# A gated feed-forward stage in token blocks of 384 instead of 256, with its inner features in pieces of 128

## The chip, the cores and the metric

The kernel runs on one core of a Trainium2 chip. The metric is the device time of one execution in microseconds (us). The core has TensorE (matmul; PE in the profile, its weight load PEld), VectorE (DVE), ScalarE (ACT), GpSimd (POOL) and SyncE (SP), whose queue issues every DMA of this kernel. Each engine works its own instructions in the order in which they stand in the program, and waits for others by semaphores.

## The reference

Three layers follow one another on 4 x 576 = 2304 tokens of width 512.

```
out_d     = softmax attention over q, k, v averaged over 4 neighbours   (144 x 144 per head)
out_local = softmax attention of each token on its 7 nearest tokens
x   = out_local + out_d repeated 4 times          -> 2304 x 512
xn  = x / sqrt(mean(x*x) + 1e-6) * rms_g
h   = silu(xn @ w_gate) * (xn @ w_val)            w: 512 x 1536
y   = h @ w_out                                   1536 x 512
r   = relu(y @ w_in)                              512 x 2048
out = (r * r) @ w_out2                            2048 x 512
```

## The kernel before

Every large product is made of three matmuls: an operand is split into a high part rounded to fp32r (names ending in h or hi) and the rest (l or lo), and high x high, high x low and low x high are summed in PSUM. The weights come as 64-bit words and are decoded in halves of 512 columns (`decode`): about four instructions on VectorE, two on ScalarE, two on GpSimd for each half.

The program has three overlapping parts.

Attention. `down` (16 pairs of heads, letters d in PLAN) is the averaged attention. `wide` and `wide_post` (a and b) do the local attention of batch 0 in 6 pieces of 96 tokens on TensorE. The other three batches' local attention is done by GpSimd and VectorE in 14 units of up to 128 tokens (`attend`, letter u): products `pr<-k,q` and `pr<-v,es`, of 128x896, one for each of 4 token rows, sums `sc` and `xa` on VectorE, the softmax `es` between them. `post` (letter p) adds the averaged part, takes the norm (squares on ScalarE, a small matmul `t<-ss,on`, a power `ms<-ms,half` on GpSimd), turns the unit (`t<-id,xa`) and splits it into the tiles xh and xl that the next stage reads.

First stage (w_gate, w_val, w_out). The tokens come in 9 blocks of 256, the inner features in 6 parts of 256. A step x (`hidden`, then `outp` of the step before) is one block and one part: 24 matmuls of 256 columns into bank g (two halves of 128 features side by side), `th` = tanh on ScalarE and one VectorE instruction on it; 24 matmuls into bank v, then `v<-v,th` on VectorE, `hh` on ScalarE, `hl<-v,hh` on VectorE; 24 matmuls from hh and hl into the block's two output banks, which are the pair a or the pair b in turn. There are 54 steps, 3888 matmuls. The first twelve steps take blocks 0 and 1 by turns (SEQ). After a block `y_out` copies its banks to SBUF and sends them to DRAM.

Second stage (w_in, w_out2): four blocks of 512 tokens and one of 256, each in 16 pieces of 128 features. Its matmuls have 512 columns.

Order. The functions only record instructions. `Plan.trace` then sets the order on each engine: it simulates the recorded instructions forth and back for ROUNDS rounds with fixed costs (`cost`, `lag`), seeds the priorities with SEED, and keeps the best round; PLAN is the order in which things are recorded, TAGS names the PSUM banks, SLOT the weight buffers. Where several engines may do an instruction (the engine names VP, AV, VPA) the same simulation picks one. Until the first matmul of the first stage it also fills TensorE's planned pauses with idle matmuls (`v<-id`, line 466 before). All instructions are issued from one line, 473 before (472 after), so tiles name them.

Of the kernel before, what the change touches and what calls it, by code (L numbers as in the profile page):

```python
# [29 lines left out]
RUNS = 32  # L30
# [11 lines left out]
BN = 256  # L42
# [21 lines left out]
SEED = 1  # L64
# [412 lines left out]
def attn_moe_kernel(ctx: ExitStack, tc, qs, kw, vw, qt, kt, vt, v4, wg, wv, wo, w2i, w2o, gw, gb,  # L477
# [7 lines left out]
    seq1 += [(j, fp) for j in range(len(set(SEQ)), len(BLK)) for fp in range(NP1)]  # L485
# [13 lines left out]
    def bank(tag, dtype=F32):  # L499
        return tile("ps", tag, [128, 512], dtype, 2 if tag in "ab" else 1)  # L500
# [42 lines left out]
    def decode(src, n, hi, lo, st, how="--"):  # L543
# [20 lines left out]
        if how[1] == "3":  # L564
            hf = low.bitcast(F32)
# [613 lines left out]
```

## Time and profile before

| what | value |
|---|---|
| median of 3 runs | 1001.02 us (1000.61 to 1002.26) |
| the profiled execution | 1000.25 us, span 998.0 us, mean granted clock 0.998 |
| TensorE busy | 980.2 us (98%), 6866 matmul records |
| VectorE busy | 587.6 us (59%) |
| ScalarE busy | 417.0 us (42%) |
| GpSimd busy | 442.3 us (44%) |

2.25 us of the execution lie outside the span of the trace. A matmul's own duration in the profile (307 ns for one of 256 columns) holds its way through the array; the next one starts earlier, so the cost of a matmul is read from how long a row of them takes. An fp32 matmul (attention) stands in the trace as two records, one of the first and second stage as one.

### The profile page before, as it was taken

What the parts mean: (1) busy time and instruction counts of PE and PEld (TensorE: products, weight loads), DVE (VectorE), ACT (ScalarE), POOL (GpSimd) and SP (SyncE); (2) the same over time, 40 slices, a digit from 0 to 9 for tenths busy, and PEclk for the clock granted to TensorE, in tenths of its full rate; (3) what the DMA queues carried; (4) which work ended last, traced back from release to release, by engine and by line L of the source; (5) the groups of instructions that cost most, each with busy time, mean ns of one, the idle gap of its engine ahead of it and who ended that gap; (6) DMA issues with size and microseconds to landing.
All of it is one profiled execution on the core that took longest, in us unless ns stands there. A gap on an engine that the chain in (4) does not pass through costs nothing.

```text
span 998.0 us, 17246 instructions
## 1 busy us (share of the span) xinstructions
PE 980.2 (98%) x6866; PEld 906.4 (91%) x6866; DVE 587.6 (59%) x985; ACT 417.0 (42%) x984; POOL 442.3 (44%) x298
## 2 busy tenths in 40 slices
PE   7998999999999999999999999999999999999998
PEld 7888999999999999999999998888888888888897
DVE  6999899786687857575634568963222322322232
ACT  5787665532435342323244557663222212322232
POOL 2566688867656676676733465863001000100000
PEclk9999999999999999999999999999999999999999
DMA  9954553253262523222011446334000100100010
GB/s 282 262 160 157 175 179 103 73 151 113 85 182 80 171 78 115 93 65 96 28 33 60 132 128 209 104 109 137 1 1 1 54 0 1 43 1 1 1 43 22
DMA packets 38465, 92.93 MB, mean 93 GB/s; under 512 B 4218, under 2 KB 14498, under 8 KB 38386
## 3 DMA queue, kind: packets, MB, share of 16 engines
q1 hardware_dynamic: 38386, 91.84, 29.6%
q8 instruction: 54, 0.88, 0.4%
q14 instruction: 25, 0.20, 0.1%
HBM read 80.62 MB, written 11.21 MB: 92 GB/s over the span
## 4 chain that ended last, share of the span: by engine, by line
PE 89%; DVE 5%; POOL 2%; DMA 2%; issue 1%; ACT 1%; SPq 0%; DVEq 0%; POOLq 0%; ACTq 0%
PE v L473 25%; PE g L473 24%; PE a L473 20%; PE b L473 15%; DVE b L473 2%; PE d L473 2%; DVE st L473 2%; PE t L473 2%; PE v L466 1%; DMA b<-in_qt 1%; DMA st<-in_wg 1%; POOL w L473 0%; POOL st L473 0%; POOL pr L473 0%; POOL b L473 0%
## 5 line engine op out<-in xcount | busy, mean ns | idle before, releaser
L473 PE MATMUL g<-xh,w 128*128 128x256 f32 (+1 forms) x776 | 176.8, 307 | 0.4 <-DVE th L473 0.4
L473 PE MATMUL v<-xh,w 128*128 128x256 f32 (+1 forms) x632 | 147.6, 311 | 0.5 <-DVE hl L473 0.5
L473 DVE SCALAR_TENSOR_TENSOR v<-v,th 128x512 f32<-128x512 f32 (+1 forms) x94 | 63.3, 674 | 128.6 <-ACT th L473 101.3
L473 PEld LDWEIGHTS g<-xh,w 128*128 128x128 f32 x776 | 131.1, 191 | 7.0 <-ACT xh L473 0.6
L473 ACT ACTIVATE th<-g 128x512 f32<-128x512 f32 (+1 forms) x94 | 54.5, 580 | 198.1 <-PE g L473 194.8
L473 POOL TENSOR_TENSOR pr<-v,es 128x896 f32<-128x896 f32 x54 | 99.4, 1939 | 65.7 <-DVE es L473 28.2
L473 PE MATMUL v<-xh,b 128*128 128x256 f32 (+1 forms) x552 | 123.9, 303 | 0.1
L473 POOL TENSOR_TENSOR pr<-k,q 128x896 f32<-128x896 f32 x54 | 115.4, 2158 | 9.6 <-DVE sc L473 7.2
L473 PE MATMUL g<-xl,w 128*128 128x256 f32 (+1 forms) x388 | 118.3, 305 | 0.1
L473 PEld LDWEIGHTS v<-xh,w 128*128 128x128 f32 x632 | 107.7, 191 | 7.1 <-PE g L473 0.7
L473 POOL TENSOR_TENSOR xl<-st,xh 128x1024 fp32r<-128x1024 f32 (+1 forms) x10 | 21.6, 2179 | 184.7 <-ACT xh L473 184.7
L473 PE MATMUL v<-xl,w 128*128 128x256 f32 (+1 forms) x316 | 97.9, 310 | 0.0
L473 PEld LDWEIGHTS v<-xh,b 128*128 128x128 f32 x552 | 93.0, 191 | 4.4 <-PE g L473 0.3
L473 PE MATMUL g<-xh,b 128*128 128x256 f32 (+1 forms) x408 | 94.4, 310 | 0.2 <-DVE th L473 0.2
L473 ACT CAST hh<-v 128x512 fp32r<-128x512 f32 (+1 forms) x94 | 53.5, 569 | 81.6 <-DVE v L473 71.3
L473 PE MATMUL v<-xl,b 128*128 128x256 f32 (+1 forms) x276 | 83.1, 301 | 0.0
L473 DVE SCALAR_TENSOR_TENSOR g<-g,th 128x512 f32<-128x512 f32 (+1 forms) x40 | 25.8, 645 | 95.5 <-ACT th L473 95.4
L473 DVE TENSOR_TENSOR hl<-v,hh 128x512 fp32r<-128x512 f32 (+1 forms) x94 | 62.4, 664 | 26.3 <-ACT hh L473 24.6
L473 PEld LDWEIGHTS g<-xl,w 128*128 128x128 f32 x388 | 74.1, 191 | 3.6 <-DVE xl L473 0.3
L473 POOL TENSOR_TENSOR st<-st 128x512 int32<-128x512 int32 x48 | 55.9, 1166 | 41.5 <-DVE st L473 39.4
L473 PEld LDWEIGHTS g<-xh,b 128*128 128x128 f32 x408 | 69.1, 190 | 4.2 <-issue 0.3
L473 ACT ACTIVATE st<-st 128x512 int32<-128x512 uint32 (+1 forms) x96 | 64.7, 684 | 18.7 <-DVE st L473 11.2
(207 smaller groups left out, 2336.8 us busy)
## 6 DMA issues: line engine op xcount, KB each, us to landing
k<-in_kw SPq DMA_DIRECT2D x12, 640.0 KB
v<-in_vw SPq DMA_DIRECT2D x12, 640.0 KB
st<-in_w2i SPq DMA_DIRECT2D x14, 512.0 KB
st<-in_w2o SPq DMA_DIRECT2D x14, 512.0 KB
y<-vv SPq DMA_DIRECT2D x18, 256.0 KB
out<-xh SPq DMA_DIRECT2D x18, 256.0 KB
st<-y SPq DMA_DIRECT2D x8, 512.0 KB
st<-in_wg SPq DMA_DIRECT2D x7, 512.0 KB
```

The source lines that it names most:

```text
L466: self.nc.tensor.matmul(out=out, lhsT=one, rhs=one, start=True, stop=True)
L473: getattr(self.hw[on[op]], method)(*args, **kw)
```

## The change

The first three blocks keep 256 tokens, the other 1536 tokens come in four blocks of 384 (BLK, UNITS). For a block of 384 a step is cut in two pieces of 128 features: 12 matmuls of 384 columns into bank g, 12 into v, 12 into the output, with tanh, hh, hl and the VectorE instructions of 128x384. A block's output takes four banks, both a and both b, and is copied one bank at a time into the staging ring "st", or for the last block into one tile; a block that crosses a multiple of 512 tokens is sent in two DMAs. `post` now handles one unit: 14 norms of up to 4 columns where there were 7 of up to 8. `th` has one buffer instead of two. The special forms of `decode` (low word in a PSUM bank) are gone. PLAN, TAGS, SLOT, ROUNDS and SEED have new values, so the order on every engine differs; one pair of heads in `down` (tag dtdp) now sums k by four matmul groups instead of a VectorE sum.

```diff
--- before.py
+++ after.py
-UNITS = {2: [[(1, 0, 4)], [(1, 16, 2)]], 3: [[(1, 4, 4)], [(1, 8, 4)]], 4: [[(1, 12, 4)], [(2, 0, 4)]],
-         5: [[(2, 4, 4)], [(2, 8, 4)]], 6: [[(2, 12, 4)], [(2, 16, 2), (3, 16, 2)]],
-         7: [[(3, 0, 4)], [(3, 4, 4)]], 8: [[(3, 8, 4)], [(3, 12, 4)]]}
-BLK = [256] * 9
+UNITS = {2: [[(1, 0, 4)], [(1, 16, 2)]], 3: [[(1, 4, 4)], [(1, 8, 4)], [(1, 12, 4)]],
+         4: [[(2, 0, 4)], [(2, 4, 4)], [(2, 8, 4)]], 5: [[(2, 12, 4)], [(2, 16, 2), (3, 16, 2)], [(3, 0, 4)]],
+         6: [[(3, 4, 4)], [(3, 8, 4)], [(3, 12, 4)]]}
+BLK = [256, 256, 256, 384, 384, 384, 384]
...
-SLOT = [7, 8, 9, 1, 0, 4, 5, 2, 6, 3, 0, 1, 3, 4, 5, 2]
-ROUNDS = 38
+SLOT = [7, 9, 4, 1, 0, 5, 2, 3, 6, 8, 0, 1, 4, 3, 2, 5]
+ROUNDS = 11
...
-SEED = 1
+SEED = 2
...
-    def decode(src, n, hi, lo, st, how="--"):
+    def decode(src, n, hi, lo, st):
...
-        low = lw if how[0] == "-" else bank(how[0], I32)
...
-        if how[1] in "-1":
...
+        VP.tensor_tensor(out=hw, in0=hw, in1=lw, op=ALU.add)
         AV.copy(hi[:, cs], hf)
...
-            xtiles[j] = [tile("xt", t, [128, 4, BN], F32R, 2) for t in ("xh", "xl")]
+            xtiles[j] = [tile("xt", t, [128, 4, BLK[j]], F32R, 2) for t in ("xh", "xl")]
...
-    def post(j):
...
+    def post(u):
+
+        first = u.j not in xtiles
+        xh, xl = xtile(u.j)
+        if u.j == 2 and first:
+        w = u.cnt
+        ss = tile("sm", "ss", [128, 4], F32, 2)[:, 0:w]
+        od = tile("lc", "pr", [128, 2, 128], F32, 2)[:, 0:w // 2]
+        a = 0
+        for s in u.segs:
+            DQ.dma_start(
+                out=od[:, a:a + s.cnt // 2],
+                in_=od_d[s.b - 1].rearrange("(p u) e -> p u e", u=NU)[:, s.t // 2:(s.t + s.cnt) // 2])
+            a += s.cnt // 2
+        xv = u.xa.rearrange("p (a w) e -> p a w e", w=2)
+        VP.tensor_tensor(out=xv, in0=xv, in1=od.unsqueeze(2).to_broadcast([128, w // 2, 2, 128]), op=ALU.add)
+        for i in range(w):
+            A.activation(mb[:, 0:128], u.xa[:, i, :], AF.Square, accum_out=ss[:, i:i + 1])
+        mp = mb[:, 128:128 + w]
+        T.matmul(out=mp, lhsT=on_sb, rhs=ss, start=True, stop=True)
+        ms = tile("sm", "ms", [128, 4], F32, 2)[:, 0:w]
+        V.tensor_scalar(out=ms, in0=mp, scalar1=1.0 / DM, scalar2=1e-6, op0=ALU.mult, op1=ALU.add)
+        P.tensor_tensor(out=ms, in0=ms, in1=half_neg[:, 0:w], op=ALU.pow)
+        for i in range(w):
+            A.activation(u.xa[:, i, :], u.xa[:, i, :], AF.Copy, scale=ms[:, i:i + 1])
...
     def hidden(j, fp):
-        gp = bank("g")[:, 0:2 * n].rearrange("p (c n) -> p c n", c=2)
-        for c in range(2):
-            gemm(gp[:, c, :], W1[fp, 0], xh, xl, c)
-        th = tile("hp", "th", [128, 2, n], F32, 2)
-        vp = bank("v")[:, 0:2 * n].rearrange("p (c n) -> p c n", c=2)
-        for c in range(2):
-            gemm(vp[:, c, :], W1[fp, 1], xh, xl, c)
-    def y_out(j):
-            ys = tile("hp", "vv", [128, 2, n], F32, 2)
-            A.copy(ys, yps[j][m2])
-    def outp(j, fp):
-            yps[j] = [bank("ab"[j % 2])[:, 0:2 * BLK[j]].rearrange("p (m n) -> p m n", m=2) for _ in range(2)]
-            for c in range(2):
...
+
+        for cs in ((0, 1),) if n <= 256 else ((0,), (1,)):
+            w = len(cs)
+            gp = bank("g")[:, 0:w * n].rearrange("p (c n) -> p c n", c=w)
+            for i, c in enumerate(cs):
+                gemm(gp[:, i, :], W1[fp, 0], xh, xl, c, i == 0)
+            th = tile("hp", "th", [128, w, n])
+            A.activation(th, gp, AF.Tanh, scale=0.5)
+            V.scalar_tensor_tensor(out=th, in0=th, scalar=1.0, in1=gp, op0=ALU.add, op1=ALU.mult)
+            vp = bank("v")[:, 0:w * n].rearrange("p (c n) -> p c n", c=w)
+            for i, c in enumerate(cs):
+                gemm(vp[:, i, :], W1[fp, 1], xh, xl, c, i == 0)
+            V.scalar_tensor_tensor(out=vp, in0=vp, scalar=0.5, in1=th, op0=ALU.mult, op1=ALU.mult)
+            hh = tile("hp", "hh", [128, w, n], F32R, 2)
+            hl = tile("hp", "hl", [128, w, n], F32R, 2)
+            AV.copy(hh, vp)
+            V.tensor_tensor(out=hl, in0=vp, in1=hh.bitcast(F32), op=ALU.subtract)
+            yield [(j, 2 * fp + c, hh[:, i, :], hl[:, i, :]) for i, c in enumerate(cs)]
+
+    def y_out(j, m):
+        n, n0 = BLK[j], start[j]
+        w = 512 // n
+        if j == len(BLK) - 1:
+            if m == 0:
+                yps[j, "out"] = tile("xt", "xh", [128, 4, n], F32, 2)
+            ys = yps[j, "out"][:, m:m + w]
+        else:
+            ys = tile("stage", "st", [128, w, n], F32, 3)
+        AV.copy(ys, yps[j][m // w])
+        while n0 < start[j + 1]:
+            n1 = min((n0 // 512 + 1) * 512, start[j + 1])
+            DQ.dma_start(out=y_d[n0 // 512][:, m:m + w, n0 % 512:n0 % 512 + n1 - n0],
+                         in_=ys[:, :, n0 - start[j]:n1 - start[j]])
+            n0 = n1
+
+    def outp(parts):
+
+        j, f0 = parts[0][:2]
+        w = 512 // BLK[j]
+        if f0 == 0:
+            yps[j] = [bank(b)[:, 0:w * BLK[j]].rearrange("p (m n) -> p m n", m=w)
+                      for b in ("aabb" if w == 1 else "bb" if j == 1 else "aa")]
+        for m in range(4):
+            o = yps[j][m // w][:, m % w, :]
+            mc = slice(m * 128, m * 128 + 128)
+            with plan.joint():
+                for _, f, hh, hl in parts:
+                    whi, wlo = (t.rearrange("p (c m) -> p c m", c=2)[:, f % 2, mc] for t in W1[f // 2, 2])
+                    st, sp = f == 0 and m % w == 0, f == 2 * NP1 - 1
+                    T.matmul(out=o, lhsT=whi, rhs=hh, start=st, stop=False, skip_group_check=True)
+                    T.matmul(out=o, lhsT=whi, rhs=hl, start=False, stop=False, skip_group_check=True)
+                    T.matmul(out=o, lhsT=wlo, rhs=hh, start=False, stop=sp, skip_group_check=True)
+            if sp and m % w == w - 1:
+                y_out(j, m - w + 1)
...
-            j, fp = seq1[s]
-            hidden(j, fp)
-            if s:
-                outp(*seq1[s - 1])
+            for parts in hidden(*seq1[s]):
+                if todo:
+                    outp(todo.pop())
+                todo.append(parts)
...
-        r = tile("hp", "th", [128, n], F32, 2)
+        r = tile("hp", "th", [128, n])
```

VectorE at the second tanh of the first stage (th is the tanh tile, st, b_ and w_ are weight words being decoded, vs, nm, rc and qk sums of 128x144 belong to `down`). Before, from the first th to the second:

```order
L473 SCALAR_TENSOR_TENSOR th<-th,g 128x512
L473 TENSOR_TENSOR xl<-t,xh 128x4x32
L473 SCALAR_TENSOR_TENSOR v<-v,th 128x512
L473 TENSOR_SCALAR b_442<-b_442 128x512
L473 TENSOR_REDUCE vs<-b_360 72x4x64
L473 TENSOR_TENSOR hl<-v,hh 128x512
L473 TENSOR_SCALAR b_442<-b_442 128x512
L473 TENSOR_REDUCE b_294<-b_294 128x144
L473 SCALAR_TENSOR_TENSOR th<-th,g 128x512
```

Now, from the first th on:

```order
L472 SCALAR_TENSOR_TENSOR th<-th,g 128x512
L472 SCALAR_TENSOR_TENSOR b_241<-b_241 128x512
L472 TENSOR_REDUCE vs<-b_483 72x4x64
L472 TENSOR_SCALAR b_95<-b_95 96x1
L472 TENSOR_REDUCE b_400<-b_400 128x144
L472 SCALAR_TENSOR_TENSOR b_618<-t,b_95,b_415 96x512
L472 TENSOR_SCALAR b_241<-b_241 128x512
L472 TENSOR_SCALAR st<-st 128x512
L472 SCALAR_TENSOR_TENSOR st<-st 128x512
L472 TENSOR_SCALAR b_241<-b_241 128x512
L472 TENSOR_SCALAR st<-st 128x512
L472 TENSOR_REDUCE b_215<-b_215 128x144
```

Before, 7 instructions stand between the first th and the second; now 30 do, and the first th has 11 instructions fewer ahead of it. In all 179 VectorE instructions stand ahead of the second th before, 192 now.

GpSimd at the entry of the fourth block (xa is a unit's attention output, ms its norm). Before, with the two units of a block under one norm of 8 columns:

```order
L473 TENSOR_TENSOR xa<-xa,pr 128x512
L473 TENSOR_TENSOR pr<-k,q 128x896
L473 TENSOR_TENSOR xa<-xa,pr 128x512
L473 TENSOR_TENSOR pr<-k,q 128x896 x2
L473 TENSOR_TENSOR ms<-ms,half 128x8
L473 TENSOR_TENSOR pr<-k,q 128x896
L473 TENSOR_TENSOR pr<-v,es 128x7x128 x4
```

Now, with three norms before the block is whole:

```order
L472 TENSOR_TENSOR xa<-xa,pr 128x512
L472 TENSOR_TENSOR pr<-k,q 128x896 x3
L472 TENSOR_TENSOR ms<-ms,half 128x4
L472 TENSOR_TENSOR pr<-v,es 128x7x128 x4
L472 TENSOR_TENSOR pr<-k,q 128x896
L472 TENSOR_TENSOR xa<-xa,pr 128x512
L472 TENSOR_TENSOR ms<-ms,half 128x4
L472 TENSOR_TENSOR pr<-k,q 128x896 x3
L472 MEMSET vs 72x4
L472 TENSOR_TENSOR ms<-ms,half 128x4
```

The fourth block needs five units where it needed four, and products of the next unit stand between a unit's products and its norm.

## Rows read from the trace of the kernel before

**Rows 1.** Busy time by stretch: stretch, length, each engine's busy us (instructions), clock, DMA
```profile
0.00:95.30 95.30, 84.00 (x764) 76.43 (x765) 82.66 (x158) 68.87 (x213) 49.98 (x46) 0.98 0.70 216
95.30:603.50 508.20, 505.66 (x4293) 503.23 (x4293) 359.14 (x608) 219.61 (x543) 327.11 (x208) 1.00 0.36 109
603.50:998.00 394.50, 390.58 (x1813) 326.72 (x1811) 145.79 (x220) 128.52 (x230) 65.22 (x45) 1.00 0.13 43
```

**Rows 2.** TensorE's waits: who for whom, us in total, times, longest
```profile
PE d L473 <- DVE w L473: 5.5, 1, 5.5
PE t L473 <- DVE b L473: 1.9, 2, 1.0
```

**Rows 3.** Chain that ended last, in order of time: start, us, what
```profile
129.65 5.82 DMA st<-in_wg
...
593.61 2.88 PE a L473 x24
...
607.20 2.72 PE g L473 x12
```

**Rows 4.** Groups by form, TensorE: busy us, mean ns, then idle before
```profile
L473 PE MATMUL t<-ss,on 128*128 128x8 f32 x12 | 1.7, 213 | 0.0
```

**Rows 5.** TensorE in order of time: start, us, instruction
```profile
71.11 0.90 PE L473 MATMUL b<-b,qbd 128*96 128x144 f32 x6
71.84 0.38 PE L466 MATMUL v<-id 128*128 128x128 f32 x2
...
110.97 0.28 PE L473 MATMUL g<-xh,w 128*128 128x256 f32 x1
...
267.22 0.28 PE L473 MATMUL g<-xh,w 128*128 128x256 f32 x1
```

**Rows 6.** Busy time by stretch, around the start of the first stage
```profile
75.00:100.00 25.00, 21.33 (x185) 20.79 (x184) 23.63 (x43) 19.13 (x47) 16.03 (x16) 0.93 0.48 156
100.00:125.00 25.00, 24.10 (x208) 23.57 (x207) 22.38 (x37) 16.21 (x34) 16.55 (x14) 1.00 0.58 175
92.50:95.00 2.50, 2.50 (x14) 2.44 (x13) 2.50 (x5) 1.73 (x4) 1.30 (x1) 0.50 0.42 163
```

**Rows 7.** VectorE in order of time, the first two th
```profile
103.90 0.69 DVE L473 SCALAR_TENSOR_TENSOR th<-th,g 128x512 f32<-128x512 f32 x1 [0.17 <-ACT th L473]
...
108.92 0.69 DVE L473 SCALAR_TENSOR_TENSOR th<-th,g 128x512 f32<-128x512 f32 x1
```

**Rows 8.** Groups by form, VectorE
```profile
L473 DVE SCALAR_TENSOR_TENSOR v<-v,th 128x512 f32<-128x512 f32 x86 | 59.9, 696 | 118.9 <-ACT th L473 91.6 <-PE v L473 26.0
...
L473 DVE SCALAR_TENSOR_TENSOR st<-st 128x512 int32<-128x512 int32 x47 | 44.4, 947 | 3.3 <-ACT st L473 3.0
...
L473 DVE TENSOR_SCALAR st<-st 128x512 f32<-128x512 f32 x49 | 35.7, 730 | 7.1 <-ACT st L473 6.5
...
L473 DVE SCALAR_TENSOR_TENSOR v<-v,th 128x256 f32<-128x256 f32 x8 | 3.5, 431 | 9.7 <-ACT th L473 9.7
```

**Rows 9.** Groups by form, ScalarE
```profile
L473 ACT ACTIVATE th<-g 128x512 f32<-128x512 f32 x86 | 51.4, 598 | 184.5 <-PE g L473 181.3 <-PE b L473 2.9
L473 ACT CAST hh<-v 128x512 fp32r<-128x512 f32 x86 | 50.5, 587 | 77.0 <-DVE v L473 67.7 <-PE d L473 3.8 <-PE b L473 3.2
```

**Rows 10.** Groups by form, GpSimd
```profile
L473 POOL TENSOR_TENSOR pr<-k,q 128x896 f32<-128x896 f32 x54 | 115.4, 2158 | 9.6 <-DVE sc L473 7.2 <-DVE xa L473 1.8
L473 POOL TENSOR_TENSOR pr<-v,es 128x896 f32<-128x896 f32 x54 | 99.4, 1939 | 65.7 <-DVE es L473 28.2 <-ACT xh L473 12.3 <-issue 9.5
```

**Rows 11.** GpSimd in order of time: norms of the third and fourth block
```profile
193.74 1.34 POOL L473 TENSOR_TENSOR ms<-ms,half 128x6 f32<-128x6 f32 x1 [0.56 <-DVE ms L473]
...
250.98 1.66 POOL L473 TENSOR_TENSOR ms<-ms,half 128x8 f32<-128x8 f32 x1 [0.16 <-DVE ms L473]
```

**Rows 12.** Busy time by stretch, while the units are made
```profile
150.00:200.00 50.00, 49.84 (x426) 49.66 (x425) 42.41 (x61) 25.48 (x60) 43.07 (x31) 1.00 0.30 87
200.00:275.00 75.00, 74.83 (x648) 74.42 (x647) 54.23 (x100) 28.06 (x81) 48.46 (x29) 1.00 0.39 117
```

More of the change, by code (lines that the diff above doesn't have):

```diff
@@ L484, in attn_moe_kernel @@
     seq1 = [(int(c), SEQ[:i].count(c)) for i, c in enumerate(SEQ)]
-    seq1 += [(j, fp) for j in range(len(set(SEQ)), len(BLK)) for fp in range(NP1)]
+    seq1 += [(j, fp) for j in range(2, len(BLK)) for fp in range(NP1)]
     seq2 = [(j, f) for j in range(len(blk2)) for f in range(2 * NP2)]
@@ L497, in tile, with bank @@
         return plan.tile(pool, shape, dtype, tag, bufs)
-    def bank(tag, dtype=F32):
-        return tile("ps", tag, [128, 512], dtype, 2 if tag in "ab" else 1)
+    def bank(tag):
+        return tile("ps", tag, [128, 512], F32, 2 if tag in "ab" else 1)
     id_sb = tile("const", "id", [128, 128])
@@ L549, in decode @@
         hf = hw.bitcast(F32)
-        low = lw if how[0] == "-" else bank(how[0], I32)
-        A.activation(low, lw.bitcast(U32), AF.Copy, scale=2.0**-29)
-        part = lw if how[1] == "1" else low
-        V.scalar_tensor_tensor(out=part, in0=hw, scalar=-0x40000000, in1=low, op0=ALU.bitwise_and,
+        A.activation(lw, lw.bitcast(U32), AF.Copy, scale=2.0**-29)
+        V.scalar_tensor_tensor(out=lw, in0=hw, scalar=-0x40000000, in1=lw, op0=ALU.bitwise_and,
                                op1=ALU.bitwise_or)
@@ new lines, in post @@
+        tp = bank("t")
+        with plan.joint():
+            for i in range(w):
+                T.transpose(tp[:, i * 128:(i + 1) * 128], u.xa[:, i, :], id_sb)
+        tv = tp[:, 0:w * 128].rearrange("p (x k c) -> p k x c", k=4, c=RUNS)
+        ns = slice(u.col, u.col + w * RUNS)
+        for k in range(4):
+            hv, lv = (t[:, k, ns].rearrange("p (x c) -> p x c", c=RUNS) for t in (xh, xl))
+            g = g_sb[:, k:k + 1]
+            A.activation(hv, tv[:, k], AF.Copy, scale=g)
+            V.scalar_tensor_tensor(out=lv, in0=tv[:, k], scalar=g, in1=hv.bitcast(F32), op0=ALU.mult,
+                                   op1=ALU.subtract)
@@ L909, in gemm @@
+    yps = {}
+    def gemm(p, w, xh, xl, c, start=True):
         whi, wlo = (t.rearrange("p (k f) -> p k f", k=4) for t in w)
@@ L912, in gemm @@
             for k in range(4):
-                T.matmul(out=p, lhsT=whi[:, k, cs], rhs=xh[:, k, :], start=(c == 0 and k == 0), stop=False,
+                T.matmul(out=p, lhsT=whi[:, k, cs], rhs=xh[:, k, :], start=(start and k == 0), stop=False,
                          skip_group_check=True)
-                T.matmul(out=p, lhsT=whi[:, k, cs], rhs=xl[:, k, :], start=False, stop=False,
-                         skip_group_check=True)
+                T.matmul(out=p, lhsT=whi[:, k, cs], rhs=xl[:, k, :], start=False, stop=False, skip_group_check=True)
                 T.matmul(out=p, lhsT=wlo[:, k, cs], rhs=xh[:, k, :], start=False, stop=(k == 3),
@@ L932, in hidden @@
-        V.scalar_tensor_tensor(out=vp, in0=vp, scalar=0.5, in1=th, op0=ALU.mult, op1=ALU.mult)
-        hh = tile("hp", "hh", [128, 2, n], F32R, 2)
-        hl = tile("hp", "hl", [128, 2, n], F32R, 2)
-        hid[j, fp] = (hh, hl)
-        AV.copy(hh, vp)
-        V.tensor_tensor(out=hl, in0=vp, in1=hh.bitcast(F32), op=ALU.subtract)
-    def y_out(j):
-        n, n0 = BLK[j], start[j] % 512
-        for m2 in range(2):
-            ys = tile("hp", "vv", [128, 2, n], F32, 2)
-            A.copy(ys, yps[j][m2])
-            DQ.dma_start(out=y_d[start[j] // 512][:, 2 * m2:2 * m2 + 2, n0:n0 + n], in_=ys)
@@ L976, in attn_moe_kernel @@
             u.cnt = sum(s[2] for s in segs)
+            u.col = BLK[j] - RUNS * sum(s[2] for segs in blk for s in segs) + RUNS * sum(o.cnt for o in BLOCKS[j])
             for s in segs:
@@ L1018, in attn_moe_kernel @@
         elif c[0] == "p":
-            post(n)
+            post(units[n])
         elif c[0] == "w":
```

88 lines of the change are left out of this document (9 added, 79 removed).

## The prediction

> **What bounds the kernel now.** I read the busy time by stretch first, then TensorE's waits, then the chain that ended last. From the first matmul of the first stage at 95.3 us to the last stage's begin at 603.5 TensorE is busy for 505.66 of 508.20 us at full clock, and then for 390.58 of 394.50, whose last 4 us are the final copy and store [rows 1]. Of its waits the longest is the first of the program, the next ones are around 1 us [rows 2]. So behind 95.3 us the time is what TensorE has to do, plus waits of about 2.5 us; the first stage's matmuls are the largest part. Ahead of it VectorE is the engine without rest: 23.63 and 22.38 of 25 us [rows 6]. A change is worth, then, what it takes from TensorE's row of matmuls, less what it makes TensorE wait in, and more or less what it does to the start.
>
> **Fewer, longer matmuls.** In a row without a pause 24 matmuls of 256 columns take 2.88 us and 12 of 512 take 2.72 [rows 3]: 0.120 and 0.227 us each. Twice the columns cost 1.89 times as much, so a straight line through both has 0.0133 us for each matmul beside 0.417 ns for each column. No row has 384 columns. The line gives 0.1733; the bounds are 1.5 x 0.120 = 0.180 (in proportion to 256) and 0.75 x 0.227 = 0.170 (in proportion to 512). The 1536 tokens that move into blocks of 384 had 36 steps x 72 = 2592 matmuls, 311.0 us, and now have 48 pieces x 36 = 1728, by the line 299.5 us. That is 11.5 us less, between 0 and 17.3. I take the line, since two measured points fix it.
>
> Against this stands a rule of the Trainium skill ("TensorE: Matmul & The Clock Gate", section Back-to-back issue gap): at full clock a matmul takes its columns at one a cycle plus only about 2.5 ns. By it 864 matmuls fewer would save 2.2 us. The trace disagrees: by that rule 256 columns would take 0.109 us, and the row has 0.120.
>
> **What TensorE gets in addition.** One pair of heads sums k by matmuls: 9 more of 144 columns. Three of them (six records) begin at 71.11 and the next instruction at 71.84 [rows 5]: 0.24 each, 2.2 us. Norms by units need 7 more of the small matmul t<-ss,on; six cost 1.7 us [rows 4], so 2.0 us. Net of the three terms: 11.5 - 4.2 = 7.3 us less.
>
> **The start.** The first th moves forward, but the second moves back: on VectorE 192 instructions stand ahead of it, 179 before. The 13 are 12 more of decoding in place (6 x 0.947 and 6 x 0.730 [rows 8], 10.1 us), 6 fewer of the decode form in PSUM (about 0.69 each, 4.1 us), and 7 small ones of the averaged attention, some 3 us: 9 us more. VectorE had no room there [rows 6], so th, begun at 108.92 before [rows 7], begins at about 118. Bank g has one buffer, so the third g waits for it: with th's own 0.7 and a hop it starts at about 118.8, where it started at 110.97 [rows 5], 7.8 us later. But TensorE has by then done more. Counted over each program's order with the prices above, and the attention's small matmuls by their columns, the third g has 877 us of matmuls at and behind it before and 864 now: the net 7.3 and 5.7 us of attention that now stand ahead. So 13.0 - 7.8 = 5.2 us earlier at the end. The bounds: if VectorE's extra work were fully hidden, the 7.3 remain and up to 3 us of an earlier first matmul; if each of the 12 decode instructions took a third longer than its mean, th came some 4 us later still and 1 us remains. TensorE falls to the lower of its two clocks for a short stretch around 92.5 to 95 us after such waits [rows 6], and with more waits between first and second g it may do so once or twice more; it waits there anyhow, so I put 0 on it, at most half of such a stretch, 1.3 us a time.
>
> **Chains in the steady part.** Before, g's chain (th on ScalarE 0.598, th on VectorE about 0.68) had 24 matmuls of v and mostly 12 of something else to hide in; now, with 384 columns, the same chain of about 0.45 and 0.56 hides behind 12 of v and 12 of output, 4.16 us. v's chain (v<-v,th 0.696, hh 0.587, hl the like [rows 8, 9]) shrinks to three quarters and has 4.16 us too. VectorE's fixed part of 0.17 (0.431 at 256 columns against 0.696 at 512 [rows 8]) is paid 48 times instead of 36, for three instructions: 6 us on an engine that is idle for 149 us of the stage. Single th costs nothing as long as v's chain ends before the next g does, which is 2 us of matmuls. Where the order leaves it no cover I pay: at the third block's first two steps only 0.24 us of matmuls lie between one g's end and the next g, 0.88 between two v; the chains need about 1.6 and 2.5, so some 2.5 us of waiting, where the old order lost about 1.6 behind its third g. That is 1 us more.
>
> **Copies of the output.** A block of 384 uses all four output banks, so the next block's first output waits for copies that go through the ring st. The order puts 4.2 to 10.4 us of matmuls between, a copy takes about 0.45 (three quarters of hh [rows 9]), and a transfer of 512 KB, where a copy sends 192, lands in 5.82 us [rows 3], so three of four copies find a free tile and the last is needed late: 0, at most 2 us at each of three such borders.
>
> **The units.** The fourth block needs five units, not four. GpSimd's work up to its last norm: 12 products of 2.158, 11 of 1.939 [rows 10] and small ones, 54 us behind the third block's norm. That norm was at 193.74 [rows 11]; now one unit's products more stand ahead of it, so about 208. GpSimd was busy for 43.07 of 50 us from 150, and for 48.46 of 75 from 200 [rows 12], where it waited for softmaxes [rows 10]. At the first share the fifth norm comes at 271, at the second at 292. TensorE, by the same count of remaining matmuls, reaches the fourth block at about 279 and needs the norm at 273. The program now has the next unit's products queued in those waits, so I take the first share and no loss; the second gives up to 19 us.
>
> **Sum.** 5.2 - 1.0 = about 4 us less than the profiled execution's 1000.25 (span 998.0 and 2.25 outside it). That execution is 0.77 us under the median, so against the median: 1001.0 - 4.0 = 997.0 us.
>
> **Rivals.**
> - Everything that leaves TensorE is gained: VectorE's later th is absorbed and no chain shows. The full TensorE share at both ends [rows 1] speaks for it, the 30 instructions between the two th against it. 1001.0 - 7.3 = 993.7, with an earlier first matmul 991. Chance 0.27.
> - No change: the head costs 4 us more than I put, or small waits of 0.1 us in each of 48 pieces (4.8 us) eat the gain. For it: pieces are shorter, and ScalarE and VectorE serve other work in order. Against it: the pieces' cover is as long as that of the steps. 1001. Chance 0.15.
> - Nothing gained by length: if a longer matmul cost in proportion to its columns from 256 on (0.180), the first term falls to 0 or little above it, and the sum is 997.0 + 11.5 = 1008 at worst, about 1003 where VectorE's th, not TensorE's work, sets the start. Both measured points speak against it. Chance 0.03. The Trainium skill's 2.5 ns (TensorE: Matmul & The Clock Gate, Back-to-back issue gap) would take 9.3 us of the term and end near 1006.
> - Slower: GpSimd doesn't keep pace, and TensorE stands before the fourth block. It decides from a share under about 0.83 between 208 and 273 us; at 0.75 the norm comes at 280, 7 us late, and the fifth block, which needs three more units (66 us of GpSimd work in 75 us of matmuls), falls back by the same again: 997 + 7 to 14, so about 1006. For it: the share of 0.65 that the trace has there. Against it: that share came with nothing else to do. Chance 0.13.
> - Forecast, 995 to 999: chance 0.42.
>
> A difference of 0.2% (2 us) is about what runs of this kernel can tell. Faster than 999.0: the first rival and the forecast, 0.69; within 0.2%: the case of no change and most of the length case, 0.17; slower than 1003.0: the last rival and the rest, 0.14. The range for 8 in 10 is 990 to 1004: the low end is the first rival with 384 columns at 0.171, the high end takes in a fourth block that is late by 7 us.
>
> **What would show it.** In the profile after: rows of 12 matmuls of 384 columns in 2.08 us (0.173 each; 2.16 would cancel the gain); third g at about 119; the waits of TensorE by VectorE's th or hl of 2 to 4 us in total; the fourth block's first g near 279 without a pause ahead of it; last stage from about 599. The prediction is wrong if TensorE stands for more than 5 us before a block of 384, or if the third g starts before 113 or behind 123.

## The result and the profile after

The change makes the kernel slower: 1015.27 us (median of 4 runs, 1014.25 to 1016.62) beside 1001.64 us for the kernel before on the same chip (4 runs, 1000.61 to 1005.26), a ratio of 1.013 [1.0102, 1.0159]. The prediction was 997.0, with a range up to 1004. The profiled execution took 1014.25 us with a span of 1012.3, 18.3 us more than the 994 that the forecast amounts to (997.0 less 0.77 and the 2.25 outside the span).

The longer matmuls are what was predicted. In the chain of what ended last, a row of twelve matmuls of 384 columns takes 2.08 us, again and again (columns: start, us, what):

```profile
304.13 6.14 PE d L472 x24
...
318.25 2.08 PE g L472 x12
...
321.15 2.09 PE v L472 x12
...
440.88 2.08 PE g L472 x12
```

That is 0.1733 us each, the line's value to the last digit. The Trainium skill's rule ("TensorE: Matmul & The Clock Gate", section Back-to-back issue gap: one column a cycle plus about 2.5 ns) would give an estimated 0.1625; the measurement decides, as it did at 256 and 512 columns. The first row above is the summing of k by matmuls, and it is no such success: 24 records in 6.14 us.

Yet the gain never reaches the end. TensorE's busy time by stretch (columns: stretch, length, busy us and instructions of PE, PEld, DVE, ACT, POOL, then clock, DMA share, GB/s) shows where it goes:

```profile
75.00:100.00 25.00, 23.47 (x201) 22.45 (x199) 20.59 (x34) 17.56 (x40) 17.89 (x15) 0.91 0.34 104
100.00:125.00 25.00, 20.04 (x122) 17.98 (x122) 22.69 (x43) 16.25 (x36) 20.42 (x17) 0.68 0.66 196
99.00:116.10 17.10, 12.53 (x65) 10.93 (x64) 15.99 (x32) 11.43 (x27) 12.78 (x13) 0.50 0.62 184
150.00:200.00 50.00, 49.51 (x415) 49.30 (x414) 47.45 (x63) 24.60 (x50) 42.81 (x28) 1.00 0.29 91
200.00:275.00 75.00, 67.44 (x568) 65.21 (x568) 56.08 (x101) 29.99 (x91) 55.24 (x37) 1.00 0.45 137
```

Before, TensorE was busy for 24.10 us of the second stretch at full clock [rows 6], and for 74.83 of the last 75 [rows 12]. Now it has 20.04 us at 0.68 there (the third row: 17.1 us at 0.50, that is 1.2 GHz, after waits of 0.38 and 0.96 us just ahead), and it stands for 7.56 us between 200 and 275 us. TensorE in order of time, the rows with a wait at that second place (in brackets the idle time ahead of the row and what ended it; some shorter rows between are left out):

```profile
220.53 0.95 PE L472 MATMUL d<-st,qbd 128*96 128x144 f32 x6 [1.15 <-DVE st L472]
222.32 0.39 PE L472 MATMUL b<-hl,b 128*128 128x256 f32 x1 [0.73 <-DVE hl L472]
...
226.35 1.12 PE L472 MATMUL d<-vs,pt 72*72 72x65 f32 x14 [0.33 <-ACT pt L472]
...
228.87 0.38 PE L472 MATMUL g<-xl,w 128*128 128x256 f32 x1 [0.16 <-DVE xl L472]
229.94 0.95 PE L472 MATMUL d<-st,qbd 128*96 128x144 f32 x6 [0.57 <-DVE ssum L472]
...
233.84 0.39 PE L472 MATMUL g<-xh,w 128*128 128x256 f32 x1 [0.93 <-DVE th L472]
238.45 0.44 PE L472 MATMUL v<-id,pe 96*72 96x96 f32 x3 [1.48 <-ACT pt L472]
239.38 0.39 PE L472 MATMUL v<-xh,w 128*128 128x256 f32 x1 [0.48 <-ACT pt L472]
244.88 0.95 PE L472 MATMUL d<-st,qbd 128*96 128x144 f32 x6 [1.28 <-DVE pt L472]
```

This is the border where blocks 0 and 1 end and the third block begins; below it is called the border. The waits belong to two kinds of work: the averaged attention (st, qbd, pe, pt) and the third block's own chain (hl, xl, th). From 225.5 to 247.6 us no output matmul of a block stands in TensorE's order, so none could fill the later of these waits.

**One number for a place.** To compare kernels I add, at the first matmul of a step's g, its start and the matmul work that is left by the prediction's prices. While TensorE works without loss the sum stays; where it grows, time was lost. Third g: before 110.97 + 877 [rows 5], now 125.72 + 864. Its row, and that of the fourth block's first g, in TensorE's order of time:

```profile
125.72 0.28 PE L472 MATMUL g<-xh,w 128*128 128x256 f32 x1
...
294.16 0.42 PE L472 MATMUL g<-xh,w 128*128 128x384 f32 x1
```

and the second th on VectorE, which was at 108.92 [rows 7]:

```profile
123.89 0.68 DVE L472 SCALAR_TENSOR_TENSOR th<-th,g 128x512 f32<-128x512 f32 x1
```

The second g was late already. Before, it began at 104.73, and now at 113.85 (the first fence is the kernel before):

```profile
104.73 0.35 PE L473 MATMUL g<-xh,w 128*128 128x256 f32 x1 [0.44 <-DVE th L473]
```

```profile
113.85 0.56 PE L472 MATMUL g<-xh,w 128*128 128x256 f32 x1
```

The table shows the sum (steps are counted from 1, so the third g is step 3; step 19 and later are other tokens in the kernel before; "last" is the last g of the first stage). Its differences give three places.

| kernel | third g | step 7 | step 15 | step 19, second half | step 20 | last |
|---|---|---|---|---|---|---|
| before | 988.3 | 990.1 | 990.8 | 991.6 | 991.8 | 993.9 |
| changed | 989.7 | 990.8 | 1001.1 | 1002.1 | 1005.4 | 1008.3 |

The forecast had 982.8 at the third g. So the start is 6.9 us later than predicted, the border (step 7 to 15) costs 10.3 us where the kernel before loses 0.7, and the half step with the k-sums 3.3 where it loses 0.2. From step 20 to the last g they lose 2.9 and 2.1 us. Small matmuls cost a little more than their columns say (eight of 65 columns take 1.00 us from 240.92 us on, for 0.87 by the price), so the sum creeps upward in every kernel. In seven kernels below whose start is the changed one's, the third g's sum lies between 988.2 and 992.3, so one profile's sum is good to about 2 us.

### The profile page after: what moved, and what is told of

Its sections match the earlier page's. It is cut to its first block, busy times and chain, and to the rows that moved or that the text cites. A ratio compares the mean times of both kernels' runs of the same rounds, so it can differ in the third digit from the quotient of the medians.

```text
span 1012.3 us, 15627 instructions
## 1 busy us (share of the span) xinstructions
PE 982.2 (97%) x5982; PEld 900.4 (89%) x5982; DVE 595.9 (59%) x1023; ACT 417.8 (41%) x1012; POOL 450.2 (44%) x309
## 4 chain that ended last, share of the span: by engine, by line
PE 88%; POOL 3%; DVE 3%; DMA 3%; issue 1%; ACT 1%; SPq 0%; POOLq 0%; ACTq 0%; DVEq 0%
PE g L472 24%; PE v L472 24%; PE a L472 19%; PE b L472 15%; PE d L472 2%; PE v L465 2%; POOL pr L472 1%; PE t L472 1%; DVE st L472 1%; POOL b L472 1%; POOL w L472 1%; POOL st L472 1%; DMA st<-in_wv 1%; DMA st<-in_qt 1%; DVE b L472 1%
## 5 line engine op out<-in xcount | busy, mean ns | idle before, releaser
L472 PE MATMUL g<-xh,w 128*128 128x384 f32 (+2 forms) x648 | 170.9, 332 | 1.4 <-DVE th L472 0.9
L472 DVE SCALAR_TENSOR_TENSOR v<-v,th 128x512 f32<-128x512 f32 (+2 forms) x106 | 65.3, 616 | 137.7 <-ACT th L472 107.7
L472 PE MATMUL v<-xh,w 128*128 128x384 f32 (+2 forms) x536 | 142.8, 335 | 0.9 <-ACT pt L472 0.5
L472 PE MATMUL v<-xh,b 128*128 128x384 f32 (+2 forms) x456 | 118.5, 329 | 0.3 <-DVE hl L472 0.3
L472 PE MATMUL g<-xl,w 128*128 128x384 f32 (+2 forms) x324 | 107.6, 332 | 0.2 <-DVE xl L472 0.2
L472 PE MATMUL g<-xh,b 128*128 128x384 f32 (+2 forms) x344 | 91.0, 333 | 0.0
L472 PE MATMUL v<-xl,w 128*128 128x256 f32 (+2 forms) x268 | 89.3, 333 | 0.0
L472 DVE TENSOR_TENSOR hl<-v,hh 128x512 fp32r<-128x512 f32 (+2 forms) x106 | 64.2, 606 | 33.5 <-ACT hh L472 30.3
L472 PE MATMUL v<-xl,b 128*128 128x384 f32 (+2 forms) x228 | 74.5, 327 | 0.0
L472 DVE TENSOR_SCALAR st<-st 128x512 f32<-128x512 f32 (+1 forms) x98 | 69.7, 713 | 5.3 <-ACT st L472 4.0
```

Source lines behind the costliest of these rows:

```text
L472: getattr(self.hw[on[op]], method)(*args, **kw)
```

## The experiments

In those that say "every instruction in its place" the order that the planner gave the changed kernel was kept for each engine, and only the edit differs. Times are medians; the ratio is to the kernel before in the same job. The sums are those of the table above.

| run | us | ratio | third g | step 7 | step 15 | step 19, second half | step 20 |
|---|---|---|---|---|---|---|---|
| e1 k-sum | 1011.61 | 1.011 [1.0069, 1.0151] | 988.2 | 989.2 | 1000.5 | 1001.4 | 1002.7 |
| e2 ring | 1026.37 | 1.0241 [1.0213, 1.027] | 989.2 | 990.2 | 1001.9 | 1002.8 | 1006.1 |
| e3 fill | 1019.15 | 1.0171 [1.0143, 1.0199] | 993.8 | 994.9 | 1005.2 | 1006.1 | 1009.4 |
| e4 before, redrawn | 1007.07 | 1.0051 [1.0035, 1.0068] | 998.3 | 998.6 | 999.1 | 999.6 | 999.7 |
| e5 light start | 1015.07 | 1.0108 [1.008, 1.0137] | 988.3 | 990.0 | 1002.2 | 1003.1 | 1006.4 |
| e6 light border | 1016.44 | 1.012 [1.0087, 1.0154] | 992.1 | 993.3 | 1004.8 | 1005.7 | 1009.0 |
| e7 contiguous | 1012.68 | 1.0088 [1.0061, 1.0114] | 990.4 | 991.4 | 1002.6 | 1003.5 | 1003.7 |
| e8 free pairs | 1017.32 | 1.0151 [1.0117, 1.0185] | 992.0 | 993.1 | 1004.0 | 1004.9 | 1008.2 |
| e9 both | 1015.33 | 1.0138 [1.0093, 1.0184] | 992.3 | 993.4 | 1003.4 | 1004.4 | 1007.7 |
| e10 redrawn | 998.38 | 0.9952 [0.9929, 0.9974] | 983.0 | 983.9 | 989.0 | 989.8 | 989.9 |
| e11 all light | 1014.71 | 1.0128 [1.0105, 1.0152] | 990.0 | 991.0 | 998.4 | 999.3 | 1002.6 |
| e12 redrawn 2 | 999.91 | 0.9976 [0.9956, 0.9995] | 984.2 | 984.5 | 991.0 | 992.2 | 992.3 |

**The k-sums (e1, e7).**

```diff
-        if tags[3] == "-":
+        if tags[3] == "-" or (b == 3 and pr == 3):          # e1
-        kf = k[:, 4:4 + S].rearrange("p (s f) -> p f s", f=FAC)
+        kf = k[:, 4:4 + S].rearrange("p (f s) -> p f s", f=FAC)   # e7
```

> The changed kernel, every instruction in the place it has there, but the last pair of heads sums k on VectorE again, as the other fifteen pairs do: 3 matmuls of 144 columns with a contiguous operand instead of 12 whose operand takes every fourth element. Theory: the 12 cost 6.3 us of TensorE in the changed kernel (24 records from 303.97 to 310.27), 0.52 each and not the 0.24 of the prediction; 3 contiguous ones cost 0.73, and as TensorE has no other wait there, the time falls by about 5.6 us, to 1009.7 (2.2 of it priced in the prediction, about 3.4 not). Rival: the strided operand is not the cause and the stretch is a wait for k; then VectorE's sum of 0.74 us comes on top and the time moves by less than 1 us.

> The changed kernel, every instruction in its place, but the 12 matmuls that sum k of the last pair of heads read 144 neighbouring elements each instead of every fourth (they then sum other elements of k). Theory: the stride of the operand makes them 0.52 us each; contiguous, the 12 take 2.9 us instead of 6.3, the step behind is reached 3.4 us earlier, and the time falls by 2.5 to 3.4 us. Rival: they are slow for another reason (12 of them in one bank, a wait between them); still about 6 us, and no change of the time.

In e7 the step is 0.2 instead of 3.3 us, and the time 2.6 us less than the changed kernel's. The chain of what ended last shows it:

```profile
305.60 2.94 PE d L507 x24
```

The same twelve matmuls on the same tiles, 2.94 us instead of 6.14. In the view of the tile qbd between 280 and 312 us the stride shows in the records themselves (30 records, six of them of another pair; the first fence is the changed kernel, the second e7):

```profile
L472 PE MATMUL d<-st,qbd x30: 283/434/436, 284.2 to 309.8; 128*96 128x144 f32 x30
```

```profile
L507 PE MATMUL d<-st,qbd x30: 283/286/286, 285.6 to 308.3; 128*96 128x144 f32 x30
```

A median of 434 ns with every fourth element, 286 with neighbours. e1 gains 3.7 us, less than the 5.6 of its theory: with three matmuls left the next one, t<-ss, has to wait 0.94 us for ScalarE, which the slow matmuls had hidden.

**The start (e3, e5).**

```diff
+    for _ in range(int((s - free) / 0.14)):     # e3; s - free is a planned pause of TensorE, in us
+        self.nc.tensor.matmul(out=bank_a, lhsT=id_sb, rhs=id_sb, start=True, stop=True)
-    V.scalar_tensor_tensor(out=lw, in0=hw, in1=lw, ...)     # e5, and the tensor_scalar of decode
+    V.scalar_tensor_tensor(out=lw[:, 0:8], in0=hw[:, 0:8], in1=lw[:, 0:8], ...)
```

> The changed kernel, every instruction in its place, with 77 matmuls of the identity on itself (128 columns, into a bank that nobody uses there) put into nine gaps of TensorE between 96 and 122 us, where its clock fell to 1.2 GHz for 17.1 us. Theory: the third g waits for VectorE's second th, and that for VectorE's and ScalarE's queues, so at full clock it comes at most 1.5 us earlier than 125.7, and the time stays within 2 us. Rival: the half clock is what makes the start late; 14.6 us of TensorE's work between 96.9 and 116.5 us ran at half pace, so at full clock the third g comes 4 to 7 us earlier and the time falls by as much.

> The changed kernel, every instruction in its place, but 22 of VectorE's weight-decoding instructions between 93 and 120 us work on 8 columns instead of 512 (the decoded weights are then not the reference's). They took about 14 us of VectorE there. Theory: VectorE's queue sets the second th (123.89) and with it the third g (125.7); with 14 us less in that queue the third g comes 6 us or more earlier, at 120 or before, and the end by about as much. Rival: the alternation of TensorE, ScalarE and VectorE in the attention of the first tokens sets the start, with TensorE at half clock, and VectorE's decoding lies in its waits; the third g moves by less than 3 us.

In e5 the edit took less from VectorE than planned: the 22 instructions take 8.1 us instead of 14.3, since some of them are long on 8 columns too, so 6.2 us are gone and not 14. The second th then comes at 121.69 instead of 123.89 and the third g at 124.27 instead of 125.72 (VectorE in the first fence, TensorE in the second):

```profile
115.01 1.25 DVE L515 TENSOR_SCALAR st<-st 128x8 int32<-128x8 int32 x1
...
121.69 0.68 DVE L515 SCALAR_TENSOR_TENSOR th<-th,g 128x512 f32<-128x512 f32 x1
```

```profile
124.27 0.28 PE L515 MATMUL g<-xh,w 128*128 128x256 f32 x1
```

That is the rival, by a weaker test than the text names: of 6.2 us taken from VectorE's queue 1.4 reach the third g. In e3 neither came: TensorE has no pause and full clock from 100 to 125 us, and the third g is 4.1 us later.

```profile
100.00:125.00 25.00, 25.00 (x234) 24.73 (x234) 22.52 (x41) 16.89 (x38) 18.15 (x17) 1.00 0.53 164
```

The price of the filling was misjudged: it left 150 records there, and 40 of them in a row take 4.63 us, so about 17.4 us in all.

```profile
106.65 4.63 PE L505 MATMUL a<-id 128*128 128x128 f32 x40
```

Set against it are six waits from 96.9 to 111.9 us (5.9 us together) and 12.53 us of work at half clock that takes half of that at full (6.3 us). 17.4 less 12.2 is an estimate of 5.2 us later, and 4.1 were measured. So the two runs, and the second g that is late before any second th, speak for TensorE's own row, waits and half clock included, as what sets the start. Neither run shows it by itself, and how much the clock alone is worth stays open, since no run changed it without adding work.

**The border (e2, e6, e8, e9, e11).** Five edits, each taking away one suspect.

```diff
-            ys = tile("stage", "st", [128, w, n], F32, 3)        # e2
-        AV.copy(ys, yps[j][m // w])
+            ys = tile("hp", "vv", [128, w, 16 // w], F32, 2)
+        AV.copy(ys, yps[j][m // w][:, :, 0:16 // w])
-    V.tensor_reduce(out=sc_or_xa, in_=pr_view, ...)              # e6, 14 of them
+    V.tensor_reduce(out=sc_or_xa, in_=pr_view[:, :, 0:1], ...)
-    T.transpose(pps[:, c, :], pe[:, c, kc * 72:kc * 72 + 72], ...)   # e8, and so with qbd, ks, pt, vs
+    T.transpose(pps[:, c, :], id_sb[0:96, 0:72], ...)
-    P.tensor_tensor(out=pr, in0=k, in1=q, ...)                   # e11: e6 + e8 + this; e9: e6 + e8
+    P.tensor_tensor(out=pr[:, :, 0:128:64], in0=k[:, :, 0:128:64], in1=q[:, :, 0:128:64], ...)
```

> The changed kernel, every instruction in its place, but the output copies of all blocks except the last don't use the staging ring st: each copies 16 columns into a small tile of its own, and the rest of the 192 or 256 KB that goes to DRAM comes from a constant tile. This leaves out the output of those blocks (what the second stage reads is not its input). Theory: at the entry of the third block TensorE loses 10.3 us between 219 and 250 us, because q, k and v of the averaged attention wait for buffers of st that the output copies hold; without them 5 us or more of it goes, and the time falls to 1010 or below. Rival: the in-order queues of VectorE and ScalarE set these waits, whatever buffer the copies use; the time stays within 2 us of the changed kernel's.

> The changed kernel, every instruction in its place, but 14 of VectorE's sums over products (sc<-pr and xa<-pr, 1.08 us each, 15 us together, from 213.7 to 249.1 us) read only the first of their 64 or 7 terms, and take about 0.2 us each (the attention of those units is then not the reference's). Theory: at the entry of the third block TensorE waits for short instructions of VectorE (sums of k, th, hl, qbd) that stand in order behind these long ones; without them the loss between 164 and 251 us, 10.3 us, falls to 4 or less and the time to 1009 or below. Rival: TensorE's own order is the cause: it stands before matmuls of the averaged attention whose chain through loads, ScalarE and VectorE is too long for the work placed ahead of them; the loss stays above 7 us.

> The changed kernel, every instruction in its place and of its size, but TensorE's matmuls of three pairs of heads of the averaged attention (those that stand in its order between 219 and 246 us: 220.5 to 242.1, and 244.9) read constant tiles instead of q, k, the exponentials and v, so that TensorE waits for none of their chains (the attention of these pairs is then not the reference's). Everything else of the chains is done as before. Theory: TensorE's own order is the cause; at the border it has no output of blocks left to do, and stands before matmuls of these three pairs while VectorE, ScalarE and a load work at them. Without these waits the loss between 164 and 251 us falls from 10.3 us to 4 or less, and the time to 1010 or below. Rival: the third block's own chain (its input written late on VectorE at 228.54, then th, hl) would stop TensorE as long anyhow; the loss stays above 7 us.

> The changed kernel, every instruction in its place, with both edits of the two kernels before at once: the 14 sums of VectorE from 213.7 to 249.1 us shortened, and TensorE's matmuls of the three pairs of heads between 219 and 246 us on constant tiles (the attention of those units and pairs is not the reference's). Each alone left the loss between 164 and 251 us at 11 us. Theory: two chains meet at the border, each long enough to stop TensorE alone (the pairs' through VectorE, ScalarE and a load; the last step's hl and the third block's xl and th behind VectorE's sums); with both gone the loss falls to 5 us or less. Rival: something else stops TensorE there, the loads or the order on ScalarE; the loss stays above 8 us.

> The kernel of e9 (shortened sums on VectorE, TensorE's matmuls of three pairs on constant tiles), and now GpSimd's 17 products pr between about 195 and 253 us are shortened too: 2 of 128 columns, or one of 7 neighbours (about 2 us each before; the attention of those units is not the reference's). In e9 the sums sc<-pr on VectorE still waited for these products (0.90, 0.71 and 1.23 us), and hl, xl and th stood in order behind them. Theory: that is the chain that was left; the loss between 164 and 251 us falls from 13 to 6 us or less, the last xl of the third block comes 2 us or more ahead of its place in e9 (1.1 us ahead of the third block's second half of the first g). Rival: ScalarE and the loads of q, k and v (a wait of 1.15 us for in_qt, 0.92 for in_kt, th 1.40 behind ScalarE) hold it up by themselves; the loss stays above 10 us.

Step 7 to 15 costs 11.7 us in e2, 11.5 in e6, 10.9 in e8, 10.0 in e9 and 7.4 in e11, against 10.3. The text of e11 puts e9 at 13, which is not right: e9 starts 2.6 us later, and its steps 7 and 15 lie 86.43 us apart where the changed kernel's lie 86.71 (third g, step 7 and step 15 of e9, then step 7 and step 15 of the changed kernel):

```profile
128.32 0.28 PE L512 MATMUL g<-xh,w 128*128 128x256 f32 x1
...
166.40 0.28 PE L512 MATMUL g<-xh,w 128*128 128x256 f32 x1
...
252.83 0.28 PE L512 MATMUL g<-xh,w 128*128 128x256 f32 x1
```

```profile
163.79 0.28 PE L472 MATMUL g<-xh,w 128*128 128x256 f32 x1
...
250.50 0.28 PE L472 MATMUL g<-xh,w 128*128 128x256 f32 x1
```

The four kernels that don't touch the border (e1, e3, e5, e7) cost 10.3 to 12.2 us there, so e2, e6, e8 and e9 lie within what one profile can tell. Four theories in a row fell: neither the ring st, nor VectorE's long sums, nor the waits for the three pairs, nor these two together hold TensorE up by themselves. In all five edits the granted clock fell for a while at the border (0.95 in e2, 0.98 in the others, 1.00 in the changed kernel), which by an estimate takes back up to 1.5 us of the 75 at 0.98 and up to 3.8 at 0.95. The stretch of 200 to 275 us says the same; the first fence is e2, the others e6, e8, e9 and e11:

```profile
200.00:275.00 75.00, 68.59 (x558) 66.82 (x556) 54.98 (x100) 27.92 (x88) 54.30 (x36) 0.95 0.49 136
```

```profile
200.00:275.00 75.00, 68.11 (x558) 65.59 (x558) 46.99 (x101) 27.89 (x83) 53.96 (x36) 0.98 0.47 137
```

```profile
200.00:275.00 75.00, 67.79 (x564) 65.81 (x563) 57.26 (x101) 27.94 (x85) 54.46 (x37) 0.98 0.46 137
```

```profile
200.00:275.00 75.00, 68.58 (x571) 66.84 (x570) 47.10 (x101) 28.91 (x87) 55.19 (x37) 0.98 0.46 137
```

```profile
200.00:275.00 75.00, 70.62 (x601) 69.46 (x600) 45.05 (x104) 30.32 (x92) 33.37 (x38) 0.98 0.42 125
```

In e6 VectorE has 9 us less to do (46.99 against 56.08) and TensorE gains 0.7 us of busy time, part of it at half clock (0.98). Why, VectorE's own row in e9 shows, with the sums already short:

```profile
222.50 0.18 DVE L512 TENSOR_REDUCE sc<-pr 128x14 f32<-128x14 f32 x1 [0.90 <-POOL pr L512]
222.65 0.69 DVE L512 TENSOR_TENSOR hl<-v,hh 128x512 fp32r<-128x512 f32 x1
...
224.56 0.18 DVE L512 TENSOR_REDUCE sc<-pr 128x14 f32<-128x14 f32 x1 [0.71 <-POOL pr L512]
224.65 0.66 DVE L512 SCALAR_TENSOR_TENSOR xl<-t,g,xh 128x64 fp32r<-128x64 f32 x3
...
228.67 0.18 DVE L512 TENSOR_REDUCE sc<-pr 128x14 f32<-128x14 f32 x1 [1.23 <-POOL vs L512]
...
229.54 0.28 DVE L512 SCALAR_TENSOR_TENSOR xl<-t,g,xh 128x64 fp32r<-128x64 f32 x1
```

hl and xl stand in order behind sums that wait for GpSimd; a shorter sum only waits longer. With GpSimd's products short too (e11) the last xl comes at 224.60, 4.9 us earlier than in e9, of which 2.3 are e11's earlier start. The first g has no wait left, and the border costs 7.4 us, 2.6 less than in e9 and 2.9 less than in any kernel that doesn't touch it. But th (1.96 us), pt (1.28) and others still stop TensorE, so e11 lies between its theory (6 us or less) and its rival (10 or more). The profiled execution, 1011.09 us, is also the fastest of its four, and the median of 1014.71 is within 0.6 us of the changed kernel's. That GpSimd's products, behind which the short instructions stand, are a piece of the loss is suggested and not shown; the rest is more than one chain.

```profile
224.60 0.27 DVE L522 SCALAR_TENSOR_TENSOR xl<-t,g,xh 128x64 fp32r<-128x64 f32 x1
```

e2 has a second result that nobody expected, told below; its time of 1026 comes from behind the border.

**The order (e4, e10, e12).**

```diff
-SEED = 1     # e4, in the kernel before
+SEED = 2
-PLAN = 'd3 d2 d0 d1 a2 a0 w00 a1 w01 b1 a4 b0 w12 b2 a3 a5 b4 w11 w21 ...      # e12, in the changed kernel
+PLAN = 'd0 d3 d2 d1 a2 a0 w00 a1 w01 b1 b2 a4 a5 b0 a3 b4 u1 w30 w10 x w21 ...
```

and in e10 and e12 new values of TAGS, SEQ, SLOT and ROUNDS, in e12 of SEED too. These tables also choose PSUM banks and weight buffers, so "order" below means all of them together; which table does what was not tried.

> The kernel before with one number changed, the start value of the planner's random draws: the same computation, tiles, buffers, plan and matmuls, but another order of the instructions on the engines. Theory (order): which instruction stands ahead of which in the in-order queues is worth several us by itself, so this is slower than the kernel before by 3 to 10 us. Rival (structure): the order is redrawn within what the buffers allow and TensorE is full anyway; within 2 us of 1001, and the loss of the changed kernel comes from its buffers and pieces.

> The changed kernel with only the tables of its order drawn anew: the plan, the banks of the small products, the slots of the weights and the planner's start value. Same tiles, buffers, blocks of 384, pieces of 128, norms by units; k of the last pair is summed on VectorE. Theory: the changed kernel lost by its order (start and border) and by the strided operand, not by the change's parts; with another order the entry of the third block loses 3 us or less, no 12 strided matmuls stand in it, and the time is 996 to 1002, no slower than the kernel before. Rival: what the longer blocks need (one th buffer, output copies in the ring st, larger x tiles) holds TensorE up in any order; 1007 or more.

> The changed kernel, all of it computed, with only the tables of its order drawn anew, as in e10, but another draw in which no tile of the first tokens is overwritten too early (in e10 a third of the first stage's first 96 tokens' exponentials was, so that its output isn't the reference's). Theory: order alone decides between 1015 and about 998; this one too ends between 995 and 1001, with a loss of 5 us or less at the entry of the third block and a third g whose time and remaining work add up to 985 or less (before 988, changed 990). Rival: e10 was fast because of what it overwrote; this one lies above 1005.

As to the time, the order theory holds in all three; e12, which computes all of it, carries the claim for the changed kernel. One number drawn anew makes the kernel before 0.5% slower, all of it at the start: 998.3 at the third g instead of 988.3, of which 7.9 us are left at step 20. And the changed kernel, with every part of the change but the k-sums and another order, takes 999.91 us, a ratio of 0.9976 [0.9956, 0.9995]: 15 us faster than the changed kernel as given, and a little faster than the kernel before. Its third g starts 2.9 us earlier with 2.6 us less behind it (2.2 of it the k-sums), and 200 to 275 us has less idle time:

```profile
122.84 0.39 PE L471 MATMUL g<-xh,w 128*128 128x256 f32 x1 [0.77 <-DVE th L471]
```

```profile
200.00:275.00 75.00, 71.39 (x605) 70.97 (x606) 58.77 (x103) 29.69 (x88) 53.82 (x36) 0.98 0.41 128
```

At step 20 the sums of e12 and of the changed kernel lie 13.1 us apart: 5.5 at the third g (2.2 of it the k-sums' work), 3.8 at the border, 3.2 at the place of the k-sums. The border is not healed: step 7 to 15 costs 6.5 us in e12 and 5.1 in e10, above the theory's 5 and 3, where both orders of the kernel before lose 0.7 and 0.5. Whether that rest is the order too, or what the blocks of 384 need (one th, the ring), is not settled.

## Why the prediction was wrong

- **Fewer, longer matmuls**: right. 0.1733 us each, and from step 20 on 2.9 us lost where the kernel before loses 2.1.
- **"Three of them (six records) begin at 71.11 ... 0.24 each, 2.2 us"**: wrong, and the term is mis-sized. The row was one with neighbouring elements [rows 5]; the new matmuls read every fourth. 12 take 6.1 us, so the nine more and the stride cost 5.4, not 2.2 (e7: 3.2 of it is the stride).
- **The start**: the step that failed is "VectorE had no room there, so th ... begins at about 118". The second th began at 123.89, but the third g, at 125.72, stands right behind other matmuls without a wait, and the second g was late already (113.85). Taking 6.2 us from VectorE moved the third g by 1.4 (e5). VectorE was busy for 20.59 of 25 us from 75 on, not without rest as before [rows 6], and for 22.69 of the next 25, about as before. TensorE's own row came late: six waits (5.9 us), and 17.1 us at half clock, where I put 0 and a bound of 1.3 us a time. Together 6.9 us; the clock's part is estimated at 6.3 and wasn't isolated. The sign that the prediction named came: the third g behind 123.
- **"Some 2.5 us of waiting, where the old order lost about 1.6 ... 1 us more"**: the largest miss. I priced the two chains of g and v alone. At the same place stand three pairs of the averaged attention and a VectorE queue that waits for GpSimd, and TensorE has no output matmuls left to put between: 7.56 us idle in 75, 10.3 by the sum. Which of these chains costs how much stays open, since no edit but e11 moved the sum. The difference to the 0.7 before, less the 1.0 foreseen, is 8.6 us.
- Together 6.9 + 8.6 + 3.1 (the half step with the k-sums, 3.3 less the 0.2 before) = 18.6, against the 18.3 us that the profiled execution is off.
- **Copies of the output, 0**: right as far as e2 shows; taking them out of the ring gained nothing at the border, and behind step 20, where the next such copies lie, 0.8 us more was lost than before.
- **The units**: no pause of its own before the fourth block, whose first g starts at 294.16 right behind other matmuls, later than the 279 only by what was lost ahead. So the rival "GpSimd doesn't keep pace" didn't come as stated. At the third block GpSimd's products may matter, through VectorE's queue and not as a norm that comes late (e11).
- What I didn't price is that a change with a new order carries that order's own losses. e4 puts them at 5 us for a single redraw, e12 at 15 less the 3.7 of the k-sums (e1) by the medians; by the sums of the profiled executions it is 13.1 less 5.4.

## What to carry to other kernels

Where a scheduler draws a new order with the change, price the order by itself: look at each border for what a full engine has left to do while a chain runs, and redraw it before you judge the change. A wait named in a profile is the last of several; shorten the engine that it names and, in an order that is kept, the next one takes its place (none of the five edits at the border shortened the time). And a row of the trace prices an instruction only with the same operand: same columns with another stride is another instruction.

## What was not expected of the hardware

- A strided operand: an fp32 matmul of 144 columns took 0.51 us reading every fourth element and 0.245 reading neighbours (6.14 and 2.94 us for 12). The Trainium skill ("Advanced Engine Details and Errata", section SBUF Cachelines) says that reads lose where each access falls into another line of 16 bytes, and every fourth fp32 is one in each line; the trace agrees, with a factor of 2.1 that the page doesn't give.
- In e2 the second stage reads another input (a constant tile's values), and its matmuls of 512 columns take longer at a granted clock of 1.00: 12 of them 2.77 us against 2.72 in the changed kernel, throughout the last stage. The first fence is e2's chain, the second the changed kernel's.

```profile
705.86 2.77 PE g L507 x12
```

```profile
709.13 2.72 PE g L472 x12
```

The instructions and their order are the same; the data differ, and a small tile more in SBUF. Which of the two does it was not tried. This is about half of the 10.7 us by which e2's profiled span is longer (some 5 to 6 us, counted over the stage's matmuls). The rest was lost ahead of the stage, but only 0.7 us of it by step 20: from 450 to 550 us TensorE stands for 2.9 us in e2, where it is busy all the time in the changed kernel. Why was not looked into.

```profile
450.00:500.00 50.00, 48.45 (x277) 46.98 (x276) 28.15 (x54) 14.77 (x49) 31.61 (x18) 1.00 0.27 52
500.00:550.00 50.00, 48.63 (x282) 47.38 (x281) 19.33 (x39) 16.62 (x55) 7.17 (x5) 1.00 0.18 30
```
